# Twelve key loads as lists of 128-element rows, with strided score products

## The chip, the cores and the metric

The kernel runs on one core of one Trainium2 chip. The metric is the device time of one execution in microseconds. Before the change two runs gave 444.36 and 446.35 us, a median of 445.36 us.

## What is computed

An attention block with cached keys and values, in bf16: 8 batches (B) of 112 queries (Sq), a model width of 640 (D), 32 heads (H) of 192 elements (Dh) and 512 cached keys (Sk).

```python
q = (lambda x, *d: x.transpose(*d))((x @ wq).reshape(B, Sq, H, Dh), 0, 2, 1, 3)
scores = jnp.einsum("bhqd,bhkd->bhqk", q, k_cache) * (Dh ** -0.5)
p = _softmax(scores, axis=-1)
o = jnp.einsum("bhqk,bhkd->bhqd", p, v_cache)
return (lambda x, *d: x.transpose(*d))(o, 0, 2, 1, 3).reshape(B, Sq, H * Dh) @ wo
```

## The kernel before

**Tiling.** The heads are taken in 4 rounds of 8. One round of one batch is one load of keys (1.5 MB: 8 heads, 512 keys, 192 elements) and one of values; there are 32 of each, number i being round i // 8, batch i % 8. The work on them goes in 64 steps, step n being one half (4 heads) of load n // 2. A step makes, in this order: shifted copies of queries (`qc`, L611 to L615, on DVE), score products (`scores`, L618 to L653, on PE), row maxima on DVE (L663), exponentials on ACT (L668), a division by the row sums on DVE (L672), transposes of the probabilities on PE (L706) with copies back to SBUF (L719), the products with the values on PE (L739 and L750) and their copy on ACT (L760). Between the steps PE also makes the query projections (L590) and the output projections (L772).

**Order.** Every engine's order is written out by hand in a list: ORDER_PE, ORDER_ACT, ORDER_DVE and ORDER_SP. `Plan.run` (L35) walks a list and puts in a wait wherever an operation needs a result of another engine (L46). All transfers are issued from SP's list, in its order; a load stands behind the load ahead of it in that list even when its own buffer is free.

**Keys.** The keys stand in `kt` (L94), four slots of [128, 2, 3, 1024] per partition: load i lies in slot i % 4, and may be issued when the score products of load i - 4 are through. Loads 0 to 6 come in as they are and are transposed by PE (L561, copies L572). Loads 7 to 31, 25 of them, are transposed by the DMA on the way (`load_k`, L133 to L143, issued at L139). Such a load is read as 1024 rows (8 heads times 128) of 768 elements, which are 4 neighbouring keys of one head. The 768 elements make 6 blocks of 128: two pairs of keys (index a) of three blocks each (index m). Two keys are 384 elements, so block 0 of a pair is the even key's elements 0 to 127, block 1 the even key's last 64 on partitions 0 to 63 and the odd key's first 64 on partitions 64 to 127, and block 2 the odd key's last 128. In `kt` each block is a run of 1024 neighbouring columns, 128 for each head.

**Score products.** For each head of a step the even keys' scores are block 0 on 128 partitions plus block 1 on the lower 64, the odd keys' are block 2 plus block 1 on the upper 64. The queries stand still in PE as weights (`qr` and its shifted copy `qh`), and the keys move through: 256 columns per matmul, the head's 128 columns of pair 0 and then of pair 1. So a step has 8 matmuls on 128 partitions (L635 and L637) and 8 on 64 (L648 and L650, in pairs on the two halves of the array). Load and use are tied by the name ("K", i), for which the first products of steps 2i and 2i + 1 wait (L641).

**Values.** The values stand in `vt`, three slots, loaded without transposing (`load_v`, L145, issued at L150) when the value products of load i - 3 are through.

**Output.** The last output projections write bf16 to every second element of `accT` (view `oF`, L127), which PE's last transposes read as weights (L854).

Of the kernel before, what the change touches and what calls it, by code (L numbers as in the profile page):

```python
# [11 lines left out]
class Plan:  # L12
# [7 lines left out]
    def add(self, eng, name, deps, emit, sem=None, inc=1):  # L20
        assert name not in self.ops, name
        self.ops[name] = dict(eng=eng, deps=deps, emit=emit, sem=sem or eng, inc=inc)
# [30 lines left out]
def build_mha_kernel(nc, x, k_cache, v_cache, wq, wo, out):  # L53
    B, SQ, D = x.shape
# [3 lines left out]
    HU = 8  # L58
# [5 lines left out]
    NG = 2 * NR  # L64
    S2 = 2 * SQ
    SG = 2 * S2
    KS, VS, QS = 4, 3, 2 * LP
    NPL = 7
    scale = float(DH) ** -0.5
# [13 lines left out]
    def step_of(g, bb, qd):  # L83
        return 2 * (g // 2 * B + g % 2 * (B // 2) + bb) + qd

    with ExitStack() as es:
        def sb(name, shape, dt):
            return es.enter_context(nc.sbuf_tensor(name, shape, dt))

        wq_sb = sb("wq_sb", [128, DC, HU * DH], BF16)  # L90
        wo_sb = sb("wo_sb", [128, KB, D], BF16)
        accT = sb("accT", [128, 2, DC, SG], F32)
        xT_sb = sb("xT_sb", [128, DC, B * SQ], BF16)
        kt = sb("kt", [128, KS, 2, 3, HU * 128], BF16)  # L94
        vt = sb("vt", [128, VS, HU, 768], BF16)
        qr = sb("qr", [128, QS, 3, SG], BF16)
        qh = sb("qh", [128, 2, 2, 4, SQ], BF16)
        s_sb = sb("s_sb", [SQ, NSS, SK], F32)
        p_sb = sb("p_sb", [SQ, 8, SK], BF16)
        pT_sb = sb("pT_sb", [128, 2, 2, 2, 4 * SQ], BF16)  # L100
        oT_sb = sb("oT_sb", [128, 2, KB, SG], BF16)
        ident = sb("ident", [128, 128], BF16)
# [4 lines left out]
        ps = es.enter_context(nc.psum_tensor("ps", [128, 8, 512], F32))  # L107
# [6 lines left out]
        for i in range(1, NPL):  # L114
            flat = wo_flat[:, 0:HU * 768] if i % 2 else acc_flat[:, 3 * D:3 * D + HU * 768]
# [17 lines left out]
        def load_k(i):  # L133
            r, b = divmod(i, B)
            name = ("K", i)

            def emit(e):
                src = k_cache[b, r * HU:(r + 1) * HU].rearrange("u (r q) d -> (u r) (q d)", q=4)
                return e.dma_start_transpose(kt[:, i % KS].rearrange("p a m c -> p (a m) c"), src)  # L139
            deps = [("St", 2 * (i - KS) + 1, 3)] if i >= KS else []  # L140
            if i == KS - 1:
                deps = [("XT", c) for c in range(4)]
            add("SP", name, deps, emit, f"mK{i % KS}", 16)  # L143
# [437 lines left out]
        def q_slot(g, lp):  # L581
            return (LP * g + lp) % QS

        def q_fill(g, lp, c, bank):
            r, bh = divmod(g, 2)

            def emit(e):
                for dc in range(DC):
                    c0 = lp * 2 * DH + 128 * c
                    mm = e.matmul(ps[:, bank, 0:SG], wq_sb[:, dc, c0:c0 + 128], xT_sb[:, dc, bh * SG:(bh + 1) * SG],  # L590
                                  start=(dc == 0), stop=(dc == DC - 1))
                return mm

            def evac(e):
                return e.activation(qr[:, q_slot(g, lp), c, :], ps[:, bank, 0:SG], ACTF.Copy)  # L595

            old = [(k, step_of(g - 2, B // 2 - 1, lp // 2), *i) for k, i in (("St", (3,)), ("qc", ()))] if g > 1 else []
            rows = range(bh * SG // 128, (bh * SG + SG - 1) // 128 + 1)
            add("PE", ("Q", g, lp, c), [wq_piece[r, lp]] + [("evX", x) for x in rows], emit)
            add("ACT", ("evQ", g, lp, c), [("Q", g, lp, c)] + old, evac)  # L600

        def q_of(n):

            r, b, qd = place(n)
            i, bb = q_slot(group(n), 2 * qd), b % (B // 2)
            return qr[:, i:i + 2, :, bb * SQ:(bb + 1) * SQ]
# [11 lines left out]
        def scores(n):  # L618
            qd = n % 2
            ktb = kt[:, n // 2 % KS]  # L620
            qv = q_of(n)

            def raw(j, c):
                return qv[:, j, c, :]

            def cs(i):
                return slice((4 * qd + i) * 128, (4 * qd + i + 1) * 128)

            for j in range(2):
                def emit(e, j=j):  # L630
                    for h in range(2):
                        i = 2 * j + h
                        ev, od = (raw(j, 0), qh[:, n % 2, j, 1, :]) if h == 0 else (qh[:, n % 2, j, 2, :], raw(j, 2))
                        hs = slice(h * 256, (h + 1) * 256)
                        e.matmul(ps[0:SQ, 2 * j, hs], ev, ktb[:, :, 0, cs(i)], start=(h == 0), stop=False,  # L635
                                 skip_group_check=True)
                        mm = e.matmul(ps[0:SQ, 2 * j + 1, hs], od, ktb[:, :, 2, cs(i)], start=(h == 0), stop=False,  # L637
                                      skip_group_check=True)
                    return mm
                add("PE", ("Sm", n, j), [("qc", n), ("smax", n - 1, 2 * j), ("smax", n - 1, 2 * j + 1)] +  # L640
                    ([("evK", n // 2, 2 * qd + i, t) for i in range(2) for t in range(2)] if n // 2 < NPL else [("K", n // 2)]), emit)  # L641
            for i in range(4):
                def emit(e, i=i):
                    j, h = divmod(i, 2)
                    ev, od = ((raw(j, 1)[0:64], qh[64:128, n % 2, j, 0, :]) if h == 0 else
                              (qh[0:64, n % 2, j, 3, :], raw(j, 1)[64:128]))
                    hs = slice(h * 256, (h + 1) * 256)
                    m1 = e.matmul(ps[0:SQ, 2 * j, hs], ev, ktb[0:64, :, 1, cs(i)], start=False, stop=True,  # L648
                                  skip_group_check=True)
                    m2 = e.matmul(ps[0:SQ, 2 * j + 1, hs], od, ktb[64:128, :, 1, cs(i)], start=False, stop=True,  # L650
                                  skip_group_check=True)
                    return m1, m2
                add("PE", ("St", n, i), [], emit, ("PE", "PE2"))  # L653
# [212 lines left out]
        for n in range(NN):  # L866
            qc(n)
            scores(n)
            softmax(n)
            if n in BY_DMA:  # L870
                p_by_dma(n)
            else:
                transposes(n)
            values(n)
# [127 lines left out]
def bass_standalone__mha_block_cached__near_ridge_kernel(  # L1002
    nc: bass.Bass,
    x: bass.AP,
    k_cache: bass.AP,
    v_cache: bass.AP,
    wq: bass.AP,
    wo: bass.AP,
    out: bass.AP,
):  # L1010
    return build_mha_kernel(nc, x, k_cache, v_cache, wq, wo, out)
# [28 lines left out]
```

## Time and profile before

| | |
|---|---|
| profiled execution | 444.36 us, span 444.4 us |
| the other run | 446.35 us |
| mean granted TensorE clock | 0.996 |
| DMA moved | 122.02 MB, mean 275 GB/s |
| packets under 512 B | 164640 of 222184 |
| transposing key loads | 25 |
| steps | 64, of 8 full and 8 half score products each |

An engine's busy time is the time in which at least one of its instructions runs; matmuls overlap, so a matmul that is listed with 273 ns may follow the one before it after 109 ns, and the chain of the work that ended last, which counts from one start to the next, is the better guide to what a matmul costs. PE is the matmul engine, PEld its weight loads, DVE and ACT the vector and scalar engines, SP the queue that issues the transfers; L139 is line 139 of the kernel. A row "idle before" or "waited for" names who released the engine. The rows of DMA issues give the time from issue to landing, and SPq rows the time that an issue held SP's queue.

### The profile page before, as it was taken

Reading aid. Unit: us, or ns where it says so; the run is one execution under the profiler, and the core shown is the slowest. Engines: PE = TensorE matmul, PEld = TensorE weight load, DVE = VectorE, ACT = ScalarE, POOL = GpSimd, SP = SyncE. Lnnn points to the kernel's source line nnn. Section 1 sums busy time; section 2 is a strip of 40 time slices with the busy share of each in tenths; the row PEclk is TensorE's granted clock in tenths of the full one; section 3 lists DMA queues with packets and bytes.
Section 4 is the critical chain, followed back from the end, with each engine's and each line's share of the span. In section 5 each row is a group of like instructions: output and inputs, shape, how many; then the busy total and the mean of one; then the engine's idle time right before and its main releaser. Section 6 shows DMA issues by size and latency. Waiting matters only on the chain.

```text
span 444.4 us, 16108 instructions
## 1 busy us (share of the span) xinstructions
PE 425.1 (96%) x6805; PEld 304.5 (69%) x6805; DVE 363.2 (82%) x1165; ACT 344.4 (78%) x770; POOL 0.7 (0%) x6
## 2 busy tenths in 40 slices
PE   6998989889999999999899999999999999899995
PEld 4666666666677667777677766767667766676895
DVE  1579999879699889888989798889799888969871
ACT  3699999887678687978869688788778758965773
POOL 0000000000000000000000000000000000000000
PEclk9999999999999999999999999999999999989999
DMA  8999999998999999999999999999999999999952
GB/s 278 373 337 323 347 299 285 226 342 276 232 289 317 215 270 270 365 247 288 238 223 324 301 236 267 360 370 234 234 266 313 256 267 371 234 173 242 237 176 80
DMA packets 222184, 122.02 MB, mean 275 GB/s; under 512 B 164640, under 2 KB 222112, under 8 KB 222112
## 3 DMA queue, kind: packets, MB, share of 16 engines
q1 hardware_dynamic: 222112, 120.99, 106.6%
q8 instruction: 54, 0.88, 0.8%
q14 instruction: 18, 0.15, 0.1%
HBM read 78.22 MB, written 1.15 MB: 179 GB/s over the span
## 4 chain that ended last, share of the span: by engine, by line
PE 84%; DVE 5%; ACT 5%; DMA 4%; issue 2%; SPq 0%; ACTq 0%
PE ps L772 19%; PE ps L590 18%; PE ps L750 12%; PE ps L648 7%; PE ps L739 7%; PE ps L635 6%; PE ps L637 6%; PE ps L706 5%; DVE s_sb L663 3%; DMA wo_sb<-in_k_cache_dram 2%; PE ps L561 2%; ACT p_sb L668 2%; DMA wq_sb<-in_wq_dram 2%; ACT qr L595 1%; DVE p_sb L672 1%
## 5 line engine op out<-in xcount | busy, mean ns | idle before, releaser
L668 ACT ACTIVATE p_sb<-s_sb,nmx 112x512 bf16<-112x512 f32 x256 | 182.8, 717 | 31.6 <-DVE s_sb L663 26.8
L663 DVE TENSOR_SCALAR_CACHE_REDUCE s_sb<-ps 112x512 f32<-112x512 f32 x256 | 169.4, 684 | 29.6 <-PE ps L650 20.8
L590 PE MATMUL ps<-xT_sb,wq_sb 128*128 128x448 bf16 x480 | 102.0, 353 | 3.3 <-DMA wq_sb<-in_wq_dram 2.3
L772 PE MATMUL ps<-oT_sb,wo_sb 128*128 128x448 bf16 (+1 forms) x480 | 93.3, 341 | 0.1
L672 DVE TENSOR_SCALAR p_sb<-p_sb,rinv 112x512 bf16<-112x512 bf16 x256 | 81.3, 347 | 1.5
L590 PEld LDWEIGHTS ps<-xT_sb,wq_sb 128*128 128x128 bf16 x480 | 42.9, 98 | 41.5 <-DMA wq_sb<-in_wq_dram 2.9
L772 PEld LDWEIGHTS ps<-oT_sb,wo_sb 128*128 128x128 bf16 x480 | 44.3, 98 | 35.0 <-DVE pT_sb L719 0.5
L760 ACT ACTIVATE oT_sb<-ps 128x672 bf16<-128x672 f32 x64 | 46.3, 726 | 25.8 <-PE ps L750 25.4
L595 ACT ACTIVATE qr<-ps 128x448 bf16<-128x448 f32 x96 | 49.6, 539 | 12.7 <-PE ps L590 12.1
L750 PE MATMUL ps<-pT_sb,vt 128*128 128x112 bf16 x944 | 55.8, 215 | 2.0 <-issue 2.0
L719 ACT ACTIVATE pT_sb<-ps 128x768 bf16<-128x768 bf16 x59 | 47.0, 801 | 12.8 <-PE ps L706 12.8
L750 PEld LDWEIGHTS ps<-pT_sb,vt 128*128 128x128 bf16 x944 | 48.1, 99 | 6.3 <-issue 2.1
L668 ACT ACTIVATION_READ_ACCUMULATOR p_sb<-s_sb,nmx 112x1 f32 x256 | 49.5, 193 | 0.0
L719 DVE COPY pT_sb<-ps 128x1024 bf16<-128x1024 bf16 x59 | 40.3, 683 | 3.4 <-PE ps L706 2.6
L706 PE MATMUL ps<-ident,p_sb 64*128 64x64 bf16 (+1 forms) x1888 | 37.3, 185 | 1.2 <-issue 0.6
L706 PEld LDWEIGHTS ps<-ident,p_sb 64*128 64x128 bf16 (+1 forms) x1888 | 33.3, 94 | 5.8 <-DVE p_sb L672 2.0
L635 PE MATMUL ps<-kt,qr 128*112 128x256 bf16 x128 | 36.0, 282 | 0.9 <-ACT oT_sb L760 0.4
L637 PE MATMUL ps<-kt,qh 128*112 128x256 bf16 x128 | 35.2, 275 | 1.1 <-issue 1.1
L635 PE MATMUL ps<-kt,qh 128*112 128x256 bf16 x128 | 35.1, 274 | 0.0
L637 PE MATMUL ps<-kt,qr 128*112 128x256 bf16 x128 | 35.0, 274 | 0.0
L650 PE MATMUL ps<-kt,qh 64*112 64x256 bf16 x128 | 34.1, 291 | 0.1
L648 PE MATMUL ps<-kt,qr 64*112 64x256 bf16 x128 | 34.0, 291 | 0.0
(62 smaller groups left out, 478.6 us busy)
## 6 DMA issues: line engine op xcount, KB each, us to landing
vt<-in_v_cache_dram SPq DMA_DIRECT2D x32, 1536.0 KB, 9.0
wo_sb<-in_wo_dram SPq DMA_DIRECT2D x4, 1920.0 KB, 12.7
wq_sb<-in_wq_dram SPq DMA_DIRECT2D x14, 480.0 KB, 5.7
wo_sb<-in_k_cache_dram SPq DMA_DIRECT2D x3, 1536.0 KB, 9.3
accT<-in_k_cache_dram SPq DMA_DIRECT2D x3, 1536.0 KB, 12.7
vt<-in_k_cache_dram SPq DMA_DIRECT2D x2, 768.0 KB, 10.0
out_dram<-xT_sb SPq DMA_DIRECT2D x8, 140.0 KB, 3.2
wq_sb<-in_wq_dram SPq DMA_DIRECT2D x1, 960.0 KB, 10.6
```

The lines of the kernel that those rows point to most:

```text
L590: mm = e.matmul(ps[:, bank, 0:SG], wq_sb[:, dc, c0:c0 + 128], xT_sb[:, dc, bh * SG:(bh + 1) * SG], start=(dc == 0), stop=(dc == DC - 1))
L595: return e.activation(qr[:, q_slot(g, lp), c, :], ps[:, bank, 0:SG], ACTF.Copy)
L635: e.matmul(ps[0:SQ, 2 * j, hs], ev, ktb[:, :, 0, cs(i)], start=(h == 0), stop=False, skip_group_check=True)
L637: mm = e.matmul(ps[0:SQ, 2 * j + 1, hs], od, ktb[:, :, 2, cs(i)], start=(h == 0), stop=False, skip_group_check=True)
L648: m1 = e.matmul(ps[0:SQ, 2 * j, hs], ev, ktb[0:64, :, 1, cs(i)], start=False, stop=True, skip_group_check=True)
L663: return e.tensor_scalar(s_sb[:, a, :].rearrange("p (e c) -> p e c", e=2), ps[0:SQ, 2 * j:2 * j + 2, h * 256:(h + 1) * 256], -scale, None, ...
L668: return e.activation(p_sb[:, k, :], s_sb[:, a, :], ACTF.Exp, bias=nmx[:, k:k + 1], scale=-1.0, accum_out=rsum[:, k:k + 1])
L672: return e.tensor_scalar(p_sb[:, k, :], p_sb[:, k, :], rinv[:, k:k + 1], None, op0=ALU.mult)
L706: ends.append(e.transpose(psb[:, bank + t, i * w:(i + 1) * w], p_sb[lo:hi, (4 * n + k) % 8, q * 128:(q + 1) * 128], ident[lo:hi, lo:hi]))
L719: return e.activation(dst, src, ACTF.Copy) if j == 0 else e.tensor_copy(dst, src)
L750: mm = e.matmul(ps[:, b0 + j, 2 * h * SQ:(2 * h + 1) * SQ], vtb[:, h0 + 2 * j + h, d0:d0 + 128], pT(j, h, q), start=(q == 0), stop=(q == 3))
L772: mm = e.matmul(ps[:, bank_of["O", g, m, 0], 0:nc_], wo_sb[:, k, m * 128:(m + 1) * 128], oT_sb[:, g % 2, k, 0:nc_], start=(k == 0), stop=( ...
```

## The change

Twelve of the 25 transposing loads, numbers 9, 11, 13 and so on to 31, read their source as a list of 6144 rows of 128 elements (256 bytes), which follow each other in memory without a gap: two keys of a head are three such rows. The load writes the list's transpose to the same slot of `kt` as one run of 6144 columns. Where a block was 128 neighbouring columns per head and pair, a head now has 768 columns in the order of its key pairs, three per pair, so the columns of one block are every third. A score product must still take pair 0 of each row of four keys first and then pair 1, as the values' rows are ordered so; its 256 columns are two passes with a stride of 6 elements, 3 elements apart. The other 13 transposing loads, the values, and the four order lists stay. For the steps of the twelve loads, `keys` returns the new access; for the others it returns what stood there before.

```diff
+    LISTED = tuple(range(9, 32, 2))
...
             def emit(e):
-                src = k_cache[b, r * HU:(r + 1) * HU].rearrange("u (r q) d -> (u r) (q d)", q=4)
+                src = k_cache[b, r * HU:(r + 1) * HU]
+                if i in LISTED:
+                    src = src.rearrange("u (g k) d -> (u g) (k d)", k=2).rearrange("a (m w) -> (a m) w", w=128)
+                    return e.dma_start_transpose(kt[:, i % KS].rearrange("p a m c -> p (a m c)"), src)
+                src = src.rearrange("u (r q) d -> (u r) (q d)", q=4)
                 return e.dma_start_transpose(kt[:, i % KS].rearrange("p a m c -> p (a m) c"), src)
...
+            def keys(lo, hi, blk, i):
+                if n // 2 not in LISTED:
+                    return ktb[lo:hi, :, blk, cs(i)]
+                flat = ktb.rearrange("p a m c -> p (a m c)")[lo:hi, (4 * qd + i) * 768:(4 * qd + i + 1) * 768]
+                return flat.rearrange("p (r a m) -> p a r m", a=2, m=3)[:, :, :, blk]
...
-                        e.matmul(ps[0:SQ, 2 * j, hs], ev, ktb[:, :, 0, cs(i)], start=(h == 0), stop=False,
+                        e.matmul(ps[0:SQ, 2 * j, hs], ev, keys(0, 128, 0, i), start=(h == 0), stop=False,
                                  skip_group_check=True)
-                        mm = e.matmul(ps[0:SQ, 2 * j + 1, hs], od, ktb[:, :, 2, cs(i)], start=(h == 0), stop=False,
+                        mm = e.matmul(ps[0:SQ, 2 * j + 1, hs], od, keys(0, 128, 2, i), start=(h == 0), stop=False,
                                       skip_group_check=True)
...
-                    m1 = e.matmul(ps[0:SQ, 2 * j, hs], ev, ktb[0:64, :, 1, cs(i)], start=False, stop=True,
+                    m1 = e.matmul(ps[0:SQ, 2 * j, hs], ev, keys(0, 64, 1, i), start=False, stop=True,
                                   skip_group_check=True)
-                    m2 = e.matmul(ps[0:SQ, 2 * j + 1, hs], od, ktb[64:128, :, 1, cs(i)], start=False, stop=True,
+                    m2 = e.matmul(ps[0:SQ, 2 * j + 1, hs], od, keys(64, 128, 1, i), start=False, stop=True,
                                   skip_group_check=True)
```

## The prediction

> **What bounds the kernel now.** I read the page first: its span, the busy times and the chain of work that ended last.
>
> ```profile
> span 444.4 us, 16108 instructions
> PE 425.1 (96%) x6805; PEld 304.5 (69%) x6805; DVE 363.2 (82%) x1165; ACT 344.4 (78%) x770; POOL 0.7 (0%) x6
> PEclk9999999999999999999999999999999999989999
> DMA  8999999998999999999999999999999999999952
> PE 84%; DVE 5%; ACT 5%; DMA 4%; issue 2%; SPq 0%; ACTq 0%
> PE ps L772 19%; PE ps L590 18%; PE ps L750 12%; PE ps L648 7%; PE ps L739 7%; PE ps L635 6%; PE ps L637 6%; PE ps L706 5%; DVE s_sb L663 3%; DMA wo_sb<-in_k_cache_dram 2%; PE ps L561 2%; ACT p_sb L668 2%; DMA wq_sb<-in_wq_dram 2%; ACT qr L595 1%; DVE p_sb L672 1%
> ```
>
> Two resources look full: PE (96%) and the DMA engines (nines nearly everywhere). The chain says which of them is the bound: 84% of the span is PE matmuls, one behind another, at a full clock, and only 4% is a DMA. The score products (L635, L637, L648) hold 6 + 6 + 7 = 19% of the span in it. The next view asks where PE ever waited for a transfer: who waited for whom, PE and its weight loads, the rows that name a DMA.
>
> ```profile
> PE ps L590 <- DMA wq_sb<-in_wq_dram: 2.3, 2, 2.0
> PE ps L561 <- DMA wo_sb<-in_k_cache_dram: 1.4, 1, 1.4
> PEld ps L590 <- DMA wq_sb<-in_wq_dram: 2.9, 2, 2.1
> PEld ps L561 <- DMA wo_sb<-in_k_cache_dram: 1.5, 1, 1.5
> ```
>
> None names kt (the keys' buffer) or vt (the values'). In the chain in order of time the DMA pieces (start, length) lie before the first transposing load is issued (68.5 us, below):
>
> ```profile
> 2.27 6.76 DMA wq_sb<-in_wq_dram
> 33.96 9.34 DMA wo_sb<-in_k_cache_dram
> ```
>
> So the DMA engines are full, but with work that is early enough; PE is the bound from there on.
>
> **Part 1: the twelve listed loads.** Per load the bytes and the number of 128 x 128 blocks (48) stay; the source becomes 6144 consecutive rows of 256 bytes instead of 1024 rows cut into six blocks. What a transposing load costs now, and how early it is (issue and landing of L139 over the whole run, then SP's queue in its longest run of such issues):
>
> ```profile
> L139 SPq DMA_TRANSPOSE kt<-in_k_cache_dram x25: 6109/6834/15432, 68.5 to 386.9; - x25
> DMA to landing us min/median/max: 8.7/10.2/18.8
> ```
>
> ```profile
> 291.50 35.34 SPq L139 DMA_TRANSPOSE kt<-in_k_cache_dram  x4
> 326.88 9.62 SPq L150 DMA_DIRECT2D vt<-in_v_cache_dram  x3
> ```
>
> The four loads here are 23, 25, 24, 26 in SP's order. Load 23 is issued at 291.50; even with the longest landing of all, 18.8 us, it is there at 310.3. Its product, step 46, begins here:
>
> ```profile
> 314.79 0.28 PE L635 MATMUL ps<-kt,qr 128*112 128x256 bf16 x1
> ```
>
> That is 4.5 us after the latest landing. Behind these four stand the value loads 24 and 23, which wait in SP's queue for nothing but its turn. Value load 23 is the second of the three from 326.88. The landings of the two that start in 320 to 335 us, and the first product that needs load 23 (step 46's values):
>
> ```profile
> L150 SPq DMA_DIRECT2D vt<-in_v_cache_dram x2: 582/582/582, 326.9 to 327.5; - x2
> DMA to landing us min/median/max: 7.5/9.6/11.6
> ```
>
> ```profile
> 340.14 0.58 PE L739 MATMUL ps<-pT_sb,vt 128*64 128x112 bf16 x16
> ```
>
> Issued at 327.5, landed 11.6 us later: 339.1, 1.0 us ahead of its use. So what the list form does to the transfer has two prices. Faster, by any amount: the landing moves further ahead of a product that already doesn't wait, so I cost the gain at zero; the cover is PE's own stream. Should the list form shrink all twelve issues from 6.8 us to half, 12 x 3.4 = 41 us leave SP's queue and none leaves PE. Slower: nothing up to about 1 us for the two listed loads of this stretch together (23, 25), beyond it PE waits at step 46. I take "no slower", since block and byte counts are unchanged.
>
> **Part 2: the score products.** Instructions and their order on PE are unchanged; each step still has 16 matmuls of 256 columns. What moves is the address of a column: the moving operand was two runs of 128 neighbours, and is now, for the steps of a listed load, 256 columns 6 elements (12 bytes) apart in two passes 3 elements apart. Here is such a step, 18 (first half of load 9), in the chain in order of time (start, length, what):
>
> ```profile
> 140.13 0.11 PE ps L635
> 140.24 0.11 PE ps L637
> ...
> 140.90 0.11 PE ps L637
> 141.00 0.24 PE ps L648
> ...
> 141.47 0.11 PE ps L648
> 141.57 0.00 PE ps L650
> 141.58 0.52 PE ps L706 x28
> ```
>
> Eight full products follow at 0.11 us, then four pairs on half the rows each, a pair in one 0.11 us slot (L650 adds 0.00); the first pair's 0.24 holds a switch of about 0.13 that doesn't scale with columns. So 12 slots of 256 columns, 12 x 0.11 = 1.3 us. The 19% of the chain gives the same by another way: 0.19 x 444.4 / 64 steps = 1.3 us. Twelve loads are 24 steps: 24 x 12 x 0.109 = 31.4 us of the span hang on the rate at which PE takes its moving columns (0.109 from eight starts, (141.00 - 140.13) / 8). If that rate falls by a factor r, the span grows by 31.4 x (r - 1).
>
> No matmul of this trace has a strided moving operand, so r is bounded by the nearest rows: the weight loads, which also read columns from the same memory.
>
> ```profile
> L635 PEld LDWEIGHTS ps<-kt,qr 128*112 128x112 bf16 x128 | 16.7, 130 | 8.6 <-DVE s_sb L663 3.1 <-issue 0.8 <-ACT oT_sb L760 0.5
> L854 PEld LDWEIGHTS ps<-ident,accT 128*112 128x112 bf16 x40 | 2.9, 131 | 0.4 <-DVE accT L838 0.4
> L590 PEld LDWEIGHTS ps<-xT_sb,wq_sb 128*128 128x128 bf16 x480 | 42.9, 98 | 41.5 <-DMA wq_sb<-in_wq_dram 2.9 <-ACT kt L572 1.0 <-issue 0.6
> ```
>
> Low end: L854 reads accT's output view with every second bf16 element (4 bytes apart), and takes 131 ns against 130 for 112 neighbours. A stride costs nothing there: r = 1, 0 us. A gain is excluded: a column can't be cheaper to read apart than beside its neighbour. High ends: PE reading columns at the pace of a weight load. 128 columns in 98 ns are 196 for 256, r = 196 / 109 = 1.8, +25 us; 112 columns in 130 ns are 297 for 256, r = 2.7, +54 us. The 2.7 is the port's slowest row and the farthest from a moving stream; the free row has a stride a third of ours and a stream less than half as fast, so a delay that is hidden there (0.77 ns or more per column) needn't be at 0.43 ns. I take the middle of the two nearer ends, r = 1.4: +12.6 us.
>
> [...]
>
> Passed on: PE is the chain at these places, so I count the whole. What is late next: the row maxima (DVE L663) wait for a step's last pair, and 0.5 us more per step arrives there too, which the following PE work must wait for where the chain runs through DVE and ACT (5% + 5%); elsewhere it gives those engines time. Neither is large beside the 12.6.
>
> **Sum.** The profiled execution's own time is 444.36, its span 444.4: 444.4 + 12.6 + 0 = 457.0. The median of the two runs, 445.36, is 1.0 above it, so 458.0.
>
> **The rivals.**
> *The stride is free, and the time stays.* r = 1 as at L854: 444 to 446, since the transfers gain nothing. It decides up to r = 1.28 (8.9 us, 2%). For it: the one strided read by PE in the trace. Against: its stride is shorter and its pace slower. [...]
> *A strided column costs a weight load's.* r = 1.8 with the 98 ns row: +25, 470.5; to about r = 2, +31, 477. [...] Against: only the other port's row. With the 130 ns row: +54, 499.
> *The list is slower on the DMA queue.* If it holds SP for 6.8 us longer each, load 23 and 25 make value load 23 late by 13.6 - 1.0 = 12.6 us, and 458 comes out by another road, with PE waiting for a DMA; in other stretches SP's runs of lists are shorter, so I add nothing for them. For it: the engines are full. Against: as many bytes and blocks, from consecutive addresses.
> *The list is faster and that shows.* To win over 2% (9 us) there must be waits to remove; the four rows above are 8.1 us in all even where they overlap, and their pieces in the chain lie before any listed load.
>
> **How the numbers follow.** Likeliest, a strided read that is dearer by r = 1.2 to 1.6 (452 to 465): 0.38. Free: 0.26. Weight load's pace (465 to 477): 0.20; the 2.7 row: 0.06. Slower queue: 0.06. A gain: 0.04. Two per cent, about what a measurement of this kernel can tell from no change, is 8.9 us, 454.3. Faster is the gain, 0.04; the same is the free case and a sixth of the likeliest (r below 1.28): 0.32; slower is the rest, 0.64. The range takes in the free case and the 1.8 row: 444 to 476, which leaves out the gain, the 2.7 row and the tail of the queue's case.
>
> **What would show it.** Right: L635 and L637 split into two kinds, starts 0.11 us apart for even loads and about 0.15 for odd ones from 9 on, in the chain and in the timeline; the chain's share of the score lines rises from 19% to some 21%; issue and landing of listed loads no longer than L139's 6.8 and 10.2; still no PE row that waits for a DMA into kt or vt. Wrong: starts 0.11 apart in listed steps too (free), 0.2 or more (a load's pace), or new waits of PE for vt or kt (the queue). That listing is free for PE is what would most easily make this prediction wrong.

## The result, and the profile after

The changed kernel takes 521.95 us (median of 521.64 and 522.27) against 445.36 us: 1.170 times the time before, interval 1.158 to 1.181. The forecast was 458.0 us, range 444 to 476. The direction was right, the size far off.

The page of the changed kernel, its lines that answer to those shown of before:

```profile
span 520.5 us, 16108 instructions
PE 505.5 (97%) x6805; PEld 322.2 (62%) x6805; DVE 365.1 (70%) x1165; ACT 344.1 (66%) x770; POOL 0.7 (0%) x6
PEclk9999999999989899999889998989998998989889
DMA  8999899999998969959937975999839999928542
PE 90%; ACT 5%; issue 2%; DVE 1%; DMA 1%; SPq 0%; ACTq 0%; DVEq 0%
PE ps L783 18%; PE ps L595 17%; PE ps L659 11%; PE ps L761 11%; PE ps L646 10%; PE ps L648 9%; PE ps L750 6%; PE ps L717 5%; ACT p_sb L679 2%; PE ps L566 2%; DMA wq_sb<-in_wq_dram 1%; ACT oT_sb L771 1%; ACT kt L577 1%; ACT qr L600 1%; DVE s_sb L674 1%
```

(The lines have moved: L635, L637, L648 and L650 are now L646, L648, L659 and L661; L590 and L772 are L595 and L783; the listed load is issued at L142, the other at L144.) PE does the same 6805 matmuls, and its busy time is 80 us longer; DVE and ACT are as busy as before, in microseconds. The score lines' share of the chain has risen from 19% to 11 + 10 + 9 = 30%, where some 21% was forecast. And the clock's row, an unbroken 9 before but for one slice, has eleven eights.

This is step 18, the first listed one, in the chain in order of time:

```profile
140.24 0.34 PE ps L646
140.58 0.34 PE ps L648
...
142.62 0.34 PE ps L648
142.96 0.45 PE ps L659
...
144.09 0.34 PE ps L659
144.43 0.00 PE ps L661
144.43 0.47 PE ps L717 x27
144.90 1.97 PE ps L595 x5
```

Two things are to be seen. A strided product takes its slot for (142.96 - 140.24) / 8 = 0.340 us, not 0.109: r = 3.1. In all 24 steps of listed loads it is the same, 0.338 to 0.342 us from one start to the next. And the five projections behind the step (L595), whose data nobody touched, take 1.97 us. Before, five of them took half of that, right ahead of the same step:

```profile
139.18 0.94 PE ps L590 x5
```

The windows of the changed kernel say why (length; busy time of PE, PEld, DVE, ACT and POOL; the granted clock; DMA's share and GB/s):

```profile
140.05:144.87 4.82, 4.82 (x51) 2.17 (x49) 1.54 (x5) 2.03 (x6) 0.00 (x0) 1.00 1.05 367
144.87:148.28 3.41, 3.41 (x11) 1.38 (x11) 2.85 (x10) 1.37 (x4) 0.00 (x0) 0.50 1.18 205
148.28:152.00 3.72, 3.72 (x21) 1.92 (x20) 2.05 (x6) 2.68 (x7) 0.00 (x0) 1.00 1.45 219
```

For 3.41 us after the strided step PE is granted half its clock. The trace has twelve such stretches between 100 us and the last output, and that of the kernel before has one, at 389.6 us. To see how much each part did, I summed the time from each PE matmul's start to the next one's, less the idle part, by kind (us, one profiled execution each; the kernels of the four last columns are told below):

```
                    before   after   half_only  full_only  third   split
score products       98.1    161.5     118.1      140.6    113.7   160.5
all other matmuls   326.8    343.7     326.5      325.9    326.2   332.6
PE idle              13.6     10.6      10.0        9.9     12.1    12.9
sum                 438.5    515.8     454.6      476.4    451.9   506.1
```

From before to after: 63.4 us in the score products, 16.9 in other matmuls (the half clock), 3.0 back from PE's waits; 77.3 together, for a span that grew by 76.1.

The transfers did nothing. Issue and landing of the listed loads (L142) and of the others (L144):

```profile
L142 SPq DMA_TRANSPOSE kt<-in_k_cache_dram x12: 6222/6600/14959, 115.4 to 443.6; - x12
DMA to landing us min/median/max: 8.4/10.2/18.2
```

```profile
L144 SPq DMA_TRANSPOSE kt<-in_k_cache_dram x13: 6112/6697/12944, 69.2 to 433.1; - x13
DMA to landing us min/median/max: 8.4/10.5/14.9
```

6.6 us against 6.7 on SP's queue, and 10.2 against 10.5 to the landing: consecutive rows are no faster than rows cut into six blocks. The DMA rows that PE waits for name neither kt nor vt, as before:

```profile
PE ps L595 <- DMA wq_sb<-in_wq_dram: 1.8, 2, 1.5
PE ps L566 <- DMA wo_sb<-in_k_cache_dram: 0.3, 1, 0.3
PEld ps L595 <- DMA wq_sb<-in_wq_dram: 2.4, 2, 1.7
PEld ps L566 <- DMA wo_sb<-in_k_cache_dram: 0.4, 1, 0.4
```

One correction to what stands above: 522.27 us belongs to a span of 520.5, 1.8 us more, and the kernels below show some 2 us as well. The execution of before with the span of 444.4 was therefore most likely the one of 446.35 us, and not 444.36. The median of 445.36 us, on which the forecast of 458.0 rests, stays as it is.

### The profile page after: what moved, and what is told of

It reads as the page before. It is cut to its first block, busy times and chain, and to the rows that moved or that the text cites. A ratio compares the mean times of both kernels' runs of the same rounds, so it can differ in the third digit from the quotient of the medians.

```text
span 520.5 us, 16108 instructions
## 1 busy us (share of the span) xinstructions
PE 505.5 (97%) x6805; PEld 322.2 (62%) x6805; DVE 365.1 (70%) x1165; ACT 344.1 (66%) x770; POOL 0.7 (0%) x6
## 4 chain that ended last, share of the span: by engine, by line
PE 90%; ACT 5%; issue 2%; DVE 1%; DMA 1%; SPq 0%; ACTq 0%; DVEq 0%
PE ps L783 18%; PE ps L595 17%; PE ps L659 11%; PE ps L761 11%; PE ps L646 10%; PE ps L648 9%; PE ps L750 6%; PE ps L717 5%; ACT p_sb L679 2%; PE ps L566 2%; DMA wq_sb<-in_wq_dram 1%; ACT oT_sb L771 1%; ACT kt L577 1%; ACT qr L600 1%; DVE s_sb L674 1%
## 5 line engine op out<-in xcount | busy, mean ns | idle before, releaser
L595 PE MATMUL ps<-xT_sb,wq_sb 128*128 128x448 bf16 x480 | 105.0, 361 | 2.8 <-DMA wq_sb<-in_wq_dram 1.8
L783 PE MATMUL ps<-oT_sb,wo_sb 128*128 128x448 bf16 (+1 forms) x480 | 100.6, 360 | 0.1
L783 PEld LDWEIGHTS ps<-oT_sb,wo_sb 128*128 128x128 bf16 x480 | 46.7, 103 | 40.1 <-issue 7.7
L595 PEld LDWEIGHTS ps<-xT_sb,wq_sb 128*128 128x128 bf16 x480 | 43.7, 99 | 42.8 <-issue 3.5
L600 ACT ACTIVATE qr<-ps 128x448 bf16<-128x448 f32 x96 | 49.6, 539 | 18.5 <-PE ps L595 17.7
L761 PE MATMUL ps<-pT_sb,vt 128*128 128x112 bf16 x944 | 57.0, 217 | 0.6 <-issue 0.6
L761 PEld LDWEIGHTS ps<-pT_sb,vt 128*128 128x128 bf16 x944 | 49.4, 100 | 5.2 <-issue 0.8
L646 PE MATMUL ps<-kt,qr 128*112 128x256 bf16 x128 | 46.7, 365 | 0.5 <-ACT oT_sb L771 0.4
L646 PE MATMUL ps<-kt,qh 128*112 128x256 bf16 x128 | 46.7, 365 | 0.0
L648 PE MATMUL ps<-kt,qh 128*112 128x256 bf16 x128 | 46.7, 365 | 0.0
L648 PE MATMUL ps<-kt,qr 128*112 128x256 bf16 x128 | 46.7, 365 | 0.0
L661 PE MATMUL ps<-kt,qh 64*112 64x256 bf16 x128 | 46.3, 377 | 0.1
L659 PE MATMUL ps<-kt,qr 64*112 64x256 bf16 x128 | 46.2, 376 | 0.0
L659 PE MATMUL ps<-kt,qh 64*112 64x256 bf16 x128 | 44.3, 362 | 0.7 <-issue 0.7
L661 PE MATMUL ps<-kt,qr 64*112 64x256 bf16 x128 | 44.3, 362 | 0.0
## 6 DMA issues: line engine op xcount, KB each, us to landing
wo_sb<-in_wo_dram SPq DMA_DIRECT2D x4, 1920.0 KB, 10.2
```

The source lines that it names most:

```text
L646: e.matmul(ps[0:SQ, 2 * j, hs], ev, keys(0, 128, 0, i), start=(h == 0), stop=False, skip_group_check=True)
L648: mm = e.matmul(ps[0:SQ, 2 * j + 1, hs], od, keys(0, 128, 2, i), start=(h == 0), stop=False, skip_group_check=True)
L659: m1 = e.matmul(ps[0:SQ, 2 * j, hs], ev, keys(0, 64, 1, i), start=False, stop=True, skip_group_check=True)
L661: m2 = e.matmul(ps[0:SQ, 2 * j + 1, hs], od, keys(64, 128, 1, i), start=False, stop=True, skip_group_check=True)
L761: mm = e.matmul(ps[:, b0 + j, 2 * h * SQ:(2 * h + 1) * SQ], vtb[:, h0 + 2 * j + h, d0:d0 + 128], pT(j, h, q), start=(q == 0), stop=(q == 3))
L783: mm = e.matmul(ps[:, bank_of["O", g, m, 0], 0:nc_], wo_sb[:, k, m * 128:(m + 1) * 128], oT_sb[:, g % 2, k, 0:nc_], start=(k == 0), stop=( ...
```

## The experiments

My theory after the result: all of the loss is the strided read, directly at 0.340 us a product, and through a clock that is halved behind it. Rivals: the transfer has a share after all; any stride costs this much; the clock's loss has another cause.

**list_only: the load alone.** The twelve lists stay, the products read neighbours.

```diff
-                if n // 2 not in LISTED:
+                if True:
                     return ktb[lo:hi, :, blk, cs(i)]
```

> The twelve loads as lists, but the score products read the slot's columns as neighbours, as before (they then read other columns than theirs). Theory: the whole loss lies in the strided read, and none in the transfer; 445 us within 1 %, full products of listed steps 0.109 us apart again, clock near 1. Rival: the list also holds the DMA queue or the keys arrive late; then several us above 445 with waits of PE for kt or vt.

445.26 us (median of ten runs) against 445.63 (of thirteen) for the kernel before on the same chip; the interval of the ratio is 0.998 to 1.004, so no change is seen. PE never waits for a DMA into kt, and for one into vt once, for 0.3 us. The change to the transfer costs nothing and gives nothing, and a gain that is hidden under something else is not seen either: the issue takes as long as before (median 6.8 us).

**stride_only: the read alone.** The loads are as before; the products of the 24 steps are strided.

```diff
-                if i in LISTED:
+                if False:
                     src = src.rearrange("u (g k) d -> (u g) (k d)", k=2).rearrange("a (m w) -> (a m) w", w=128)
```

> All 25 loads in six blocks as before, and the strided access in the 24 steps (which then reads other columns than its own). Theory: 522 us as with the whole change, full products of listed steps 0.34 us apart. Rival (the transfer has a share): below 515.

522.61 us, 1.174 times (1.168 to 1.179), the whole loss, with full products 0.340 us apart. The two together settle where it lies.

**half_only and full_only: how the loss adds up.** Only one kind of product is strided, on 64 partitions (half_only, below) or on 128 (full_only, with blk == 1 in place of blk != 1).

```diff
-                if n // 2 not in LISTED:
+                if n // 2 not in LISTED or blk != 1:
```

> Twelve lists; only the products on 64 partitions are strided, those on 128 read neighbours (other columns than theirs). Slots: 24 x 4 = 96, each 0.231 us longer, 22.2 us. Theory A: the rest of the loss (11 us, other matmuls at half clock for 3.4 us at a time) comes only where strided products run for over 3 us on end; here they run for some 1.4 us, so no half-clock stretch after 100 us: 467.6 us. Theory B: the clock's loss goes with the strided time; a third of it, 3.8 us more: 471 us.

> Twelve lists; only the products on 128 partitions are strided, those on 64 read neighbours (other columns than theirs). Slots: 24 x 8 = 192, each 0.231 us longer, 44.4 us. Theory A (half clock only after strided products of over 3 us on end; here 2.7 us): 490 us, no half-clock stretch after 100 us. Theory B (the clock's loss goes with the strided time, two thirds of 11 us): 497 us.

463.29 us (1.041, 1.033 to 1.048) and 483.46 us (1.086, 1.081 to 1.091), both without a half-clock stretch before the last output (mean clock 1.000 in each profiled execution): theory A for the clock, and 4 and 7 us less than I had worked out. Step 18 of full_only, where the slow and the quick kind stand side by side:

```profile
139.82 0.34 PE ps L646
...
142.54 0.24 PE ps L659
142.78 0.00 PE ps L661
142.78 0.11 PE ps L659
```

17.7 us and 37.8 us are 55.5 together, against 76.6 for both kinds at once; a sum of parts falls short by 21 us. The table shows the two pieces that don't add: the other matmuls cost 16.9 us more only where both kinds are strided (326.8 before, 326.5 and 325.9 here), and PE's idle time gives back some 3.6 us in each of these two kernels and 3.0 with both kinds, and not in proportion. From here on I counted 86% of the strided time as visible. For these kernels a fixed 3 to 4 us would have been nearer; third and split, further down, gave back 1.5 and 0.7.

**stride2, stride4, stride8, stride16: other distances.** Loads as before; the 256 columns of a product stand s elements apart (the products then read other columns than theirs).

```diff
...
+                c0 = (4 * qd + i) * 128
+                flat = ktb.rearrange("p a m c -> p (a m c)")[lo:hi, c0:c0 + 256 * s]
+                return flat.rearrange("p (a r s) -> p a r s", a=2, s=s)[:, :, :, 0]
```

> All loads as before; in the 24 steps the 256 columns stand 4 bytes apart (other columns than the products need). Before this run: 0.109 us per product at 2 bytes, 0.340 at 12. Theory L (the cost is per 16-byte line entered; 192 lines in 0.340 us at 12 bytes are 1.77 ns each, and a product is never under 0.109): 64 lines, 0.113 us, so 446 us. Theory U (any gap costs the same): 0.340 us, 522 us. [...]

> Columns 8 bytes apart. Theory L: 128 lines, 0.227 us; 288 slots x 0.118 = 34 us, of which 86 % showed in the partial kernels, so 475 us. Theory U: 0.340 us, 522 us. [...]

> Columns 16 bytes apart, each alone on its line. Theory L: 256 lines, 0.453 us; 288 x 0.344 x 0.86 = 85 us and some 20 us of half clock, so 550 us. Theory U: 0.340 us, 522 us. [...]

> Columns 32 bytes apart (other columns than the products need). Theory L: still one line per column, so as at 16 bytes: 0.450 us per product and 584 us. Theory S: twice the bytes, 0.90 us per product, over 690 us.

Step 18 of each in the chain in order of time, first full product and first half product; the eight slots between them give the time of one. At 4, 8, 16 and 32 bytes:

```profile
141.08 0.11 PE ps L647
...
141.99 0.25 PE ps L660
```

```profile
140.04 0.22 PE ps L647
...
141.85 0.34 PE ps L660
```

```profile
141.39 0.45 PE ps L647
...
145.00 0.56 PE ps L660
```

```profile
140.28 0.46 PE ps L647
...
143.95 0.61 PE ps L660
```

0.114, 0.226, 0.451 and 0.459 us, and within 1% of that as medians over all 24 steps; the times are 444.43, 472.47, 583.85 and 584.54 us (one run each; the kernel before 442.35 to 447.22 beside them). "Any gap costs the same" is out: 4 bytes cost 0.005 us more than neighbours, and 8 bytes, with two columns in every 16 bytes, twice their 0.109 us. The last two settle that it saturates: at 16 bytes each column is alone in its 16 bytes, and twice the distance costs 2% more (0.459 us against 0.451). That makes 16 bytes the unit in which these runs can be counted; it is called a line here.

**quads: lines or bytes spanned.** The columns are 64 groups of four neighbours, a group every 48 bytes. They span as many bytes as the change's and lie on a third of its lines.

```diff
...
+                flat = ktb.rearrange("p a m c -> p (a m c)")[lo:hi, c0:c0 + 64 * 24]
+                return flat.rearrange("p (g w) -> p g w", w=24)[:, :, 0:4]
```

> All loads as before; in the 24 steps the 256 columns are 64 groups of four neighbours, a group every 48 bytes (other columns than the products need), so they span 3072 bytes like the change's but lie on 64 or so 16-byte lines in place of 192. Theory L (1.77 ns per line entered): 0.113 us per product, 446 us. Theory S (the cost goes with the bytes spanned, which the strides of 4, 6, 8, 12 and 16 bytes can't tell from lines): 0.340 us, 522 us.

```profile
140.06 0.11 PE ps L647
...
140.96 0.25 PE ps L660
```

(140.96 - 140.06) / 8 = 0.113 us, 443.81 us (one run) against 444.29 before. It is the lines that count (64 here, 192 in the change, for 0.113 and 0.340 us), and not the bytes spanned.

**third: the same lists, read at half the distance.** This kernel leaves nothing out. Columns 3 elements apart in one pass give the scores in another order of keys, and the value loads of the same numbers are arranged to match.

```diff
...
+                if i in LISTED:
+                    src = src.rearrange("u (t r q) d -> r u t (q d)", t=2, q=2)
+                    return e.dma_start(vt[:, i % VS].rearrange("p u (t c) -> p u t c", t=2), src)
...
+                return flat.rearrange("p (g m) -> p g m", m=3)[:, :, blk]
```

> Twelve lists; the products take every third column in one pass (6 bytes apart), so that the scores come in another order of keys, and the value loads of the same numbers are arranged to match (runs of two keys in place of four). Nothing is left out. Theory L: 96 lines, 0.170 us per product; 288 x 0.061 x 0.86 = 15 us, so 461 us, clock full. Theory U: 522 us. [...] If the value loads in shorter runs come late, PE rows that wait for vt show it.

```profile
141.28 0.17 PE ps L650
...
142.65 0.30 PE ps L663
```

0.171 us a product and 459.34 us, 1.033 times before (1.028 to 1.038). PE waits for vt once, for 0.3 us, as in list_only, so the values in shorter runs don't come late. The price by lines holds for a kernel that does the whole work. It is 63 us better than the change and still behind the kernel before: a cheaper stride has nothing to pay it back, since the list brings nothing.

**split: the clock.** The changed kernel, with a piece of other work between the two kinds of products of each listed step.

```diff
...
+            elif it[1] // 2 in LISTED and between(reordered[-1]):
+                last = reordered.pop()
+                reordered += [it, last, ("ST", it[1])]
...
```

> The changed kernel with nothing left out, but in each of the 24 steps the piece of PE's list that stood ahead of the step (a projection or the values' last products, about 1 us) is put between the products on 128 partitions and those on 64, so that strided products run for 2.7 and 1.4 us on end and not for 4.2. Theory A (the clock is halved when strided products fill a stretch of some 3.4 us): half-clock stretches gone, products still 0.340 us apart, 445 + 0.86 x 63 = 499 us. Theory B (the clock's loss goes with the strided time): 522 us.

512.65 us, 1.153 times (1.148 to 1.159), between the two theories. The first such step:

```profile
140.06:142.79 2.73, 2.73 (x9) 1.19 (x10) 1.83 (x6) 0.80 (x2) 0.00 (x0) 1.00 1.05 367
142.79:143.85 1.06, 1.06 (x8) 0.41 (x6) 0.00 (x0) 0.00 (x0) 0.00 (x0) 1.00 1.06 375
143.85:145.26 1.41, 1.41 (x9) 0.49 (x9) 0.00 (x0) 1.31 (x3) 0.00 (x0) 1.00 1.07 377
```

Here the clock stays whole. Three half-clock stretches are left, at 365.8, 386.3 and 430.7 us, where twelve were; the other matmuls cost 5.8 us more than before in place of 16.9. So breaking up the strided run does remove most of the clock's loss, as theory A has it. The three that are left lie behind stretches in which the strided products had company: PE stood idle for 0.33, 0.26 and 0.66 us beside them, waiting for DVE. Four other stretches, as full of strided products (79 to 80%) but with PE busy throughout, were not followed by half clock. Theory A, which counts strided products alone, doesn't cover these. That the time fell by 9.3 us and not by 23 is due to those three stretches for some 6 us, and for the rest to my 86%: in the new order PE's waits give back only 0.7 us.

## Why the prediction was wrong

*What bounds the kernel*: right. PE's chain sets the time; every added microsecond of PE showed but for 3 us.

*Part 1, the transfer at zero*: the number was right, and so was "no slower". The argument that PE's stream would cover a faster transfer was not put to the test: the loads are not faster, so there was nothing to hide. The rivals of the queue and of the gain both fall with list_only.

*Part 2, the slots*: 24 steps of 12 slots, 0.109 us each, and that the loss scales with r: right (31.4 x 2.1 = 66 us, 63.4 measured). The step that failed is the term r: 1.4 was taken, 0.340 / 0.109 = 3.1 was measured. The term of 12.6 us measured 63.4 us. Even the far end of the bounds, 2.7, was too low, and it was not "the port's slowest row" as I had it: the groups of weight loads of before have one of 64 columns in 110 ns, 1.7 ns a column, which by the same working is r = 4.0.

```profile
L739 PEld LDWEIGHTS ps<-pT_sb,vt 128*64 128x64 bf16 x944 | 25.6, 110 | 10.6 <-issue 3.1 <-ACT p_sb L668 1.6 <-ACT pT_sb L719 0.8
```

A load's time doesn't go with its columns (64, 112 and 128 take 110, 130 and 98 ns), so it gives no price per column. The step failed because the rows that bounded it were of another kind. Weight loads of neighbours say nothing about how a read slows when columns are apart; and the one strided row, L854 at 4 bytes, lies on the flat side of a limit, as stride2 shows for the moving operand (0.114 us). I read "free at 4 bytes" as half a reason for "not dear at 12", and put the middle between ends that were no ends. An unknown cost with no row of its kind should have had a wider range.

Counted in lines of 16 bytes, the products at 4, 6, 8, 12 and 16 bytes touch 64, 96, 128, 192 and 256 lines, and their 0.114, 0.171, 0.226, 0.340 and 0.451 us are 1.76 to 1.78 ns for each. A line costs about the time of four columns (4 x 0.426 ns = 1.7, from 0.109 / 256), so at 12 bytes, with four columns on three lines, r is 12/4 = 3, within 4% of the measured. At 8 bytes, two columns on a line, a product takes 0.226 us, twice its time with neighbours; at 16 bytes, one on a line, 0.451 us, four times.

*What is late next*: incomplete. I looked for the next wait in DVE and ACT, and their share of the chain did shrink, from 5% + 5% to 1% + 5%. What the sum left out, and so put at nothing without a reason, was the clock: 16.9 us, because matmuls of other lines ran at half pace behind strided steps.

*The rivals*: the one that asked for a weight load's pace came nearest (499 us with the dearer row, chance 0.06) and named a wrong cause: the cost goes by lines and not by a weight load's pace. *The chances*: slower had 0.64 and came true; the range's top of 476 us was set by the 1.8 row.

## What to carry to other kernels

Give a matmul's moving operand at least four bf16 columns in every 16 bytes that it touches; below that it cost by lines here, up to four times its time (0.226 us with two in 16 bytes, 0.451 with one, against 0.109), and PE counts as busy all the while, so that no wait row shows it: look at the distance between starts. If data must be rearranged, pay in whichever engine has idle time, and first run the cheap half alone (here the list without the read, 445 us): a transfer that isn't waited for can't repay a slower matmul. And when a bound for an unknown cost comes from another instruction or another access, treat it as a guess and not as an end of the range.

## What the runs showed of the hardware

*The price of a stride for the moving operand*, 256 bf16 columns, full clock: 0.109 us as neighbours, 0.114 at 4 bytes, 0.171 at 6, 0.226 at 8, 0.340 at 12, 0.451 at 16, 0.459 at 32; 0.113 in fours every 48 bytes.

*The read sets the pace, not the clock.* At 16 bytes the products on 64 partitions follow each other after 0.452 us at full clock and at half clock alike (22 and 18 gaps, 0.450 to 0.454), while products on neighbours go from 0.109 to 0.213 us at half clock (5 gaps in the kernel before).

*The clock behind slow reads.* In the changed kernel the half-clock stretches are 3.41 us long, and each of the twelve follows a stretch of 3.41 us of which strided products filled 80 to 100%, with PE's busy time at 100%. The share alone doesn't decide it: three stretches of 80, 86 and 91% were not followed by half clock. What filled the rest sorts them better. In eleven of the twelve it was transposes of the probabilities (L717), and all other matmuls had 0 to 3% of the stretch; in the three they had 20, 14 and 9%, and in the six of full_only with 79 to 82% they had 14 to 18%, none followed. The twelfth, with 13%, doesn't fit. Idle time goes along with half clock too: in split it stood beside the strided products, and in the kernel before, without any strided product, the one half-clock stretch follows 3.40 us in which PE was busy for 1.44. How slow the products are matters as well: at 8 bytes (0.226 us) there is no half-clock stretch before the last output, and at 16 and 32 bytes, where a strided step lasts 5.5 us, the clock's mean over the span falls to 0.894 and 0.889. So half clock, for 3.41 us at a time, followed here both a stretch in which PE was mostly idle and stretches of strided columns in which it was busy throughout. What the granted clock goes by is not shown.
